# Attention with head mixing and two MLPs: score rows twelve partitions apart, one DMA a head, and first-chunk moves on GpSimd's queue

## The chip, the cores and the metric

The kernel runs on one core of one Trainium2 chip. The metric is the device time of one execution in microseconds (us). The kernel before took 1219.67 us (median of three runs, 1219.64 to 1219.95).

## The reference

All data is float32; `scale` is 1/8.

```python
q, k, v: [4, 12, 448, 64]; w_pre, w_post: [12, 12]
scores = einsum('bhij,hg->bgij', scale * q @ k^T, w_pre)
attn = exp(scores - max(scores)); attn = attn / (sum(attn) + 1e-09)
o = einsum('bhij,hg->bgij', attn, w_post) @ v
x = o as [1792, 768]
y = ((x @ w1) * (x @ w2)) @ w3 @ w_out
h = y @ w_in;  return maximum(0.01 * h, h) @ w_out2
```

Both mixes run over the twelve heads: each mixed score is a sum over heads of the scores at the same place.

## The kernel before, in words

The attention comes first. The 448 query rows of each of the four batches are cut in chunks of 120, 120, 120 and 88, sixteen chunks in all (`order`). A chunk is worked in groups of two blocks; a block is ten query rows with all twelve heads, 120 of 128 partitions.

For each chunk and pair of heads, `qk` (L222) makes the scores on TensorE (L242) into two PSUM banks. Its inner `out` copies them to a tile `s` (L254 on VectorE, L256 on ScalarE) and calls `move` (L269) for each head: a DMA (L281) that takes a head's 120 rows from `s` to the tile `sr` (`rows_of`), where the rows of one block lie in one column slot: ten query rows, each with its heads side by side. In `sr`, query row i of head h lies on partition h + 13 i (`GAP`), save that head 11's last five rows begin again at partition 64, as 11 + 117 would be 128. So head 11 takes two DMAs and every other head one. The tile `s` is one tile for all heads in the first chunk; for the others there are five buffers in turn, one a pair of heads (L232). There are three `sr` tiles, taken in turn.

The mixing matrix `kpre` has the weights of `w_pre` for the five query rows of each half of 64 partitions; `premix` (L304, matmul L315) multiplies it with two column slots of `sr`. Partitions that hold no score must be finite, so `constants_load` (L150) clears the three `sr` tiles by memset, two on GpSimd and one, the first chunk's, on VectorE (L152). `constants` (L158) makes the masks of `kpre` and `kpost` from an identity.

Then, per step k of two groups: `tops` (L320, maxima by VectorE, L325), `softmax` (ScalarE, exp with the sum, L332), `weigh` (L337: VectorE's reciprocal, then the scaling of four blocks by that, three on GpSimd and one on VectorE, L348), `postmix` of the step before (L369) with VectorE's transposes (L384), `av` (L401, products px with v, two pairs of heads a step, four where many wait), and the premix of the next two groups. Scores are made `LEAD` = 10 groups ahead. The schedule is written by hand: each engine runs its instructions in the program's order, and each DMA is issued by the engine named, in that engine's order.

The start stands at L443 to L466. Ten pairs of heads (six of the first chunk, four of the second) go through `qk` with `early` set, so that ScalarE and VectorE share the copies. The first chunk's moves are made in halves, column slots 0 to 5 and 6 to 11 (`half`). Their issuing queues: first halves of even heads by ScalarE, of odd heads by SyncE (L260); second halves of odd heads by SyncE (L460), with the loads of the third chunk's q among them, those of even heads by GpSimd (L465). All later moves are SyncE's (L263). Between them TensorE runs matmuls on a tile of ones (`turn`, L302). After the first step SyncE loads the first batch's v, six DMAs (`v_load`, L219, called at L552).

After the attention come the two MLPs, TensorE work almost alone, in which nothing is changed. The host lays out the inputs (`kernel`); the rows of `w_pre` follow the layout of `sr`.

```python
    LEAD, GAP = 10, 13
    out=dst[r0:r0 + GAP * (n - 1) + 1:GAP, n0:n0 + w, :], in_=t[i0 * w:(i0 + n) * w, :]
    shares = (nc.scalar, nc.scalar, nc.gpsimd, nc.scalar) if last else (nc.gpsimd,) * 3 + (nc.vector,)
```

Of the kernel before, what the change touches and what calls it, by code (L numbers as in the profile page):

```python
# [12 lines left out]
ALU = mybir.AluOpType  # L13
# [9 lines left out]
def attention_moe_kernel(ctx: ExitStack, tc, qt, kt, vt, w_pre, w_post, w1, w2, w3t, w_out, w_in2, w_out2, out):  # L23
# [18 lines left out]
    IB = 10  # L42
    LEAD, GAP = 10, 13
    CH = qt.shape[-1]
# [73 lines left out]
    def attention(seam):  # L118
        with ExitStack() as es, ExitStack() as left:
# [22 lines left out]
            spare = spare.bitcast(F32)  # L142
            ident, ones, eye = (spare[:, n * P:n * P + w] for n, w in ((0, P), (1, P), (2, HQ * GAP)))
            mask = spare[:, 3 * P:3 * P + 2 * HQ].rearrange("p (n i) -> p n i", i=HQ)
# [5 lines left out]
            def constants_load():  # L150
                for i, t in sorted(rows_of.items()):
                    (nc.gpsimd if i else nc.vector).memset(t, 0.0)  # L152
                for t in (kpre, kpost, eye):
                    nc.gpsimd.memset(t, 0.0)
                for n, w in enumerate((w_pre, w_post)):
                    nc.sync.dma_start(out=wrep[:, n, :], in_=w)

            def constants():  # L158
                nc.vector.tensor_tensor(out=eye[:, :Q], in0=ident[:, :Q], in1=ident[:, Q:], op=ALU.add)
                for n, gap in enumerate((GAP, H)):  # L160
                    t = eye[:, :HQ * gap].rearrange("p (i h) -> p i h", h=gap)[:, :, :H]
                    nc.vector.tensor_reduce(out=mask[:, n], in_=t, axis=AX.X, op=ALU.max)
                nc.vector.tensor_scalar(
                    out=wrep[:, 0, :], in0=wrep[:, 0, :], scalar1=scale, scalar2=None, op0=ALU.mult
                )
                nc.vector.tensor_tensor(
                    out=kpre[:, :HR].rearrange("p (i h) -> p i h", h=H),
                    in0=mask[:, 0].unsqueeze(2).to_broadcast([P, HQ, H]),
                    in1=wrep[:, 0, :].unsqueeze(1).to_broadcast([P, HQ, H]), op=ALU.mult,
                )  # L170
                for c in range(2):
                    nc.vector.tensor_tensor(
                        out=kpost[:, c, :HH * HQ].rearrange("p (h i) -> p h i", i=HQ),
                        in0=mask[:, 1].unsqueeze(1).to_broadcast([P, HH, HQ]),
                        in1=wrep[:, 1, c * HH:(c + 1) * HH].unsqueeze(2).to_broadcast([P, HH, HQ]), op=ALU.mult,
                    )
# [42 lines left out]
            def v_load(b, p):  # L219
                nc.sync.dma_start(out=vs[:, p], in_=vt[b, p])  # L220

            def qk(b, c, p, early=False):  # L222
# [28 lines left out]
                def out():  # L251
                    for e in range(2):
                        if early and (e or (b, c) == order[0] and p % 2):
                            nc.vector.tensor_copy(t[:m, e, :], pq[e][:m])  # L254
                        else:
                            nc.scalar.activation(out=t[:m, e, :], in_=pq[e][:m], func=ACTF.Copy)  # L256
                    for e in range(2):
                        args = srt[b, c], t[:m, e, :], 2 * p + e
                        if (b, c) == order[0]:
                            move(*args, nc.sync if e else nc.scalar, 0)  # L260
                            second.append(args)
                        else:
                            move(*args, nc.sync)  # L263
# [5 lines left out]
            def move(dst, t, h, queue, half=None):  # L269

                m = t.shape[0]
                n0, w = 0, m // IB
                if half is not None:
                    m, w = m // 2, w // 2
                    n0, t = half * w, t[half * m:(half + 1) * m]
                if h < H - 1:
                    parts = [(h, 0, 2 * HQ)]
                else:
                    parts = [(h, 0, HQ), (Q, HQ, HQ)]
                for r0, i0, n in parts:  # L280
                    ends["sync"] = queue.dma_start(  # L281
                        out=dst[r0:r0 + GAP * (n - 1) + 1:GAP, n0:n0 + w, :], in_=t[i0 * w:(i0 + n) * w, :]
                    )

# [165 lines left out]
            turn(13)  # L450
            queued = []
            for k in range(LEAD):
# [4 lines left out]
                if k == 5:  # L457
                    constants()
                    for args in second[1::2]:
                        move(*args, nc.sync, 1)  # L460
                        if not queued and args[-1] > 4:
                            queued.append([q_load(*order[2], a) for a in range(2)])
                if k in (7, 9):
                    for args in second[(k - 7) * 3:][:6:2]:
                        move(*args, nc.gpsimd, 1)  # L465
            turn(6)  # L466

# [38 lines left out]
            for k in range(0, NG + 2, 2):  # L506
# [42 lines left out]
                do(k // 2, upper)  # L549
                if not k:  # L550
                    for p in range(NPAIR):
                        v_load(0, p)  # L552
                for g in done:
# [580 lines left out]
```

## Time and profile before

| | |
|---|---|
| median of the runs | 1219.67 us (1219.64 to 1219.95) |
| the profiled execution's own time | 1218.51 us |
| its span, first to last instruction | 1216.7 us |
| mean granted clock of TensorE | 0.997 |
| TensorE busy | 1198.3 us (98%) |
| VectorE busy | 885.7 us (73%) |
| ScalarE busy | 550.5 us (45%) |
| GpSimd busy | 213.0 us (18%) |

The profile is one execution; its times count from the first instruction. In its rows PE is TensorE's matmuls, PEld its weight loads, DVE VectorE, ACT ScalarE, POOL GpSimd, SP SyncE; a q behind the name is the engine's sequencer, which issues DMAs. L281 is line 281 of the kernel before. "sr<-s" reads: writes sr, from s. The idle time in brackets is that of the engine just before the row, with what ended it. Busy shares are means over stages with different limits; TensorE's matmuls are pipelined and their ends modelled, so that a busy TensorE may still be slowed.

### The profile page before, as it was taken

How to read it: one execution, taken by the hardware profiler on the slowest of the kernel's cores; microseconds unless marked ns; L12 is line 12 of the kernel's file. 1: busy time of each engine (PE TensorE's matmuls, PEld its weight loads, DVE VectorE, ACT ScalarE, POOL GpSimd, SP SyncE). 2: the span in 40 equal slices, each digit the busy share in tenths (PEclk: the TensorE clock that was granted, in tenths of full speed). 3: DMA queues.
4: the chain of work that ended last, by engine and by line, in shares of the span. 5: the costliest groups of instructions: out<-in, count | busy, mean ns of one | idle time of the engine just before them, and what ended most of it. 6: DMA issues, size and time to landing. Idle time of an engine off the chain costs nothing.

```text
span 1216.7 us, 22474 instructions
## 1 busy us (share of the span) xinstructions
PE 1198.3 (98%) x8782; PEld 986.5 (81%) x8782; DVE 885.7 (73%) x1525; ACT 550.5 (45%) x1118; POOL 213.0 (18%) x169
## 2 busy tenths in 40 slices
PE   8999999999999999999999999999999999999998
PEld 5355555555579999998899999999999999999998
DVE  5687787888889988547895868567776657476572
ACT  3677776866655454323454342352233334323120
POOL 5566767666410000000000000000000000000000
PEclk9999999999999999999999999999999999999999
DMA  6767867756867756589674626063342221212012
GB/s 198 235 197 205 219 188 209 207 169 186 262 222 254 241 177 189 171 288 352 217 240 136 221 92 207 27 221 115 95 131 65 65 70 52 72 34 73 26 53 91
DMA packets 135998, 196.82 MB, mean 162 GB/s; under 512 B 26724, under 2 KB 115036, under 8 KB 135892
## 3 DMA queue, kind: packets, MB, share of 16 engines
q1 hardware_dynamic: 132048, 192.72, 49.8%
q10 hardware_dynamic: 3556, 2.02, 0.6%
q8 instruction: 69, 1.13, 0.4%
q0 software_dynamic: 288, 0.65, 0.2%
q14 instruction: 37, 0.30, 0.1%
HBM read 114.57 MB, written 42.07 MB: 129 GB/s over the span
## 4 chain that ended last, share of the span: by engine, by line
PE 84%; DVE 8%; ACT 4%; DMA 3%; issue 1%; ACTq 0%; POOL 0%; SPq 0%; DVEq 0%; POOLq 0%
PE pm L597 29%; PE po L611 19%; PE pp L908 17%; DVE ap L384 6%; PE px L401 6%; PE pw L669 6%; PE po L369 4%; ACT e L332 3%; DMA sr<-s 3%; PE pq L242 2%; PE pm L315 2%; DVE mx L325 1%; PE turn L302 1%; ACT s L256 0%; DVE e L348 0%
## 5 line engine op out<-in xcount | busy, mean ns | idle before, releaser
L597 PE MATMUL pm<-x,ws 128*128 128x384 f32 (+1 forms) x1152 | 233.9, 364 | 0.0
L597 PEld LDWEIGHTS pm<-x,ws 128*128 128x128 f32 x1152 | 208.7, 188 | 24.5 <-issue 0.6
L348 POOL TENSOR_SCALAR e<-e,sm 128x448 f32<-128x448 f32 x128 | 184.5, 1454 | 132.6 <-DVE sm L342 116.0
L332 ACT ACTIVATE e<-pm,mx 128x448 f32<-128x448 f32 x180 | 111.7, 632 | 78.2 <-DVE mx L325 71.6
L384 DVE STREAM_TRANSPOSE ap<-po 128x512 f32<-128x512 f32 (+3 forms) x216 | 115.8, 594 | 24.7 <-PE po L369 24.1
L908 PE MATMUL pp<-t,w 128*128 128x448 f32 x576 | 124.5, 368 | 0.0
L611 PE MATMUL po<-ws,g 128*128 128x384 f32 x672 | 117.2, 334 | 0.0
L611 PE MATMUL po<-wo,g 128*128 128x384 f32 x672 | 117.2, 334 | 0.0
L908 PEld LDWEIGHTS pp<-t,w 128*128 128x128 f32 x576 | 108.1, 188 | 10.9
L611 PEld LDWEIGHTS po<-wo,g 128*128 128x128 f32 x672 | 116.6, 188 | 0.2
L611 PEld LDWEIGHTS po<-ws,g 128*128 128x128 f32 x672 | 116.6, 188 | 0.0
L325 DVE TENSOR_REDUCE mx<-pm 128x1 f32<-128x448 f32 x180 | 98.6, 603 | 8.9 <-PE pm L315 8.9
L100 ACT ACTIVATE wc<-wr 128x768 f32<-128x768 f32 (+1 forms) x72 | 61.7, 859 | 87.5 <-DMA wr<-in_moe_w_dram 33.6
L908 PE MATMUL pp<-b,w 128*128 128x448 f32 x432 | 95.6, 368 | 0.0
L401 PEld LDWEIGHTS px<-ap,vs 96*64 96x64 f32 (+1 forms) x1536 | 77.7, 136 | 22.0 <-ACT e L332 16.3
L618 DVE TENSOR_TENSOR acc<-po,acc 128x384 f32<-128x384 f32 x84 | 45.4, 554 | 66.9 <-PE po L611 66.8
L256 ACT ACTIVATE s<-pq 120x448 f32<-120x448 f32 (+1 forms) x179 | 83.1, 561 | 18.2 <-PE pq L242 9.9
L315 PE MATMUL pm<-sr,kpre 64*64 64x448 f32 x720 | 84.0, 554 | 7.0 <-DMA sr<-s 5.1
L401 PE MATMUL px<-ap,vs 96*64 96x120 f32 (+3 forms) x1536 | 87.6, 266 | 3.0 <-ACT e L332 1.3
L369 PE MATMUL po<-e,kpost 64*32 64x512 f32 (+1 forms) x1472 | 89.2, 586 | 1.4 <-POOL e L348 1.2
L908 PEld LDWEIGHTS pp<-b,w 128*128 128x128 f32 x432 | 81.0, 188 | 8.0
L72 ACT ACTIVATE ws<-wc 128x768 fp32r<-128x768 f32 (+1 forms) x64 | 49.7, 788 | 69.6 <-PE po L611 45.2
(106 smaller groups left out, 1577.5 us busy)
## 6 DMA issues: line engine op xcount, KB each, us to landing
sr<-s SPq DMA_DIRECT2D x121, 210.0 KB
wr<-in_moe_w_out_dram SPq DMA_DIRECT2D x24, 768.0 KB
wr<-in_moe_w_dram SPq DMA_DIRECT2D x16, 768.0 KB
wr<-in_moe_w_in_dram SPq DMA_DIRECT2D x16, 768.0 KB
wr<-in_moe_w_dram SPq DMA_DIRECT2D x16, 512.0 KB
sr<-s SPq DMA_DIRECT2D x44, 157.5 KB
vs<-in_v_dram SPq DMA_DIRECT2D x24, 256.0 KB
kept_w<-wc SPq DMA_DIRECT2D x16, 384.0 KB
```

What stands on the lines that cost most here:

```text
L256: nc.scalar.activation(out=t[:m, e, :], in_=pq[e][:m], func=ACTF.Copy)
L315: nc.tensor.matmul(pms[ns[s % len(ns)]][half:half + Q], kpre[rows], sr[rows, 2 * t + g, :], start=True, stop=True,)
L325: nc.vector.tensor_reduce(out=mxs[n], in_=pms[n], axis=AX.X, op=ALU.max, negate=True)
L332: ends["act"] = nc.scalar.activation(out=e[:, i], in_=pms.pop(n), func=ACTF.Exp, bias=mxs.pop(n), scale=1.0, accum_out=sm[:, i:i + 1])
L348: ends["dve" if eng is nc.vector else "pool"] = eng.tensor_scalar(out=e[:, i], in0=e[:, i], scalar1=rc[:, i:i + 1], scalar2=None, op0=ALU.mult
L369: nc.tensor.matmul(po[g][32 * r:32 * (r + 1), :m], kpost[rows, x], e[rows, :m, JS[r]:JS[r] + P], start=True, stop=True,)
L384: ends["dve"] = nc.vector.transpose(out=dst, in_=po[g][:, i0:i1])
L401: nc.tensor.matmul(px[e * D:(e + 1) * D, r, :nw].rearrange("p (n i) -> p n i", i=HQ), vs[rows, p, jc, e, :], ap[rows, x, :ns, jc, h * HQ:( ...
L597: nc.tensor.matmul(dst, wt[:, a, kk, :], x[kk][:, c, c0:c0 + w], start=(i == 0), stop=(i == len(steps) - 1))
L611: nc.tensor.matmul(po, g[m][:, a, t * P:(t + 1) * P], wts[m][:, c, cs], start=(m == 0 and j == 0), stop=(m == FQ - 1 and j == 2),)
L669: nc.tensor.matmul(pw, wt[:, x, kk, :], wos[kk][y][:, cs], start=(kk == 0 and j == 0), stop=(kk == KF - 1 and j == 2),)
L908: nc.tensor.matmul(dst, w[:, i, a, kk, :], b[:, kk, c, :], start=(kk == 0 and j == 0), stop=(kk == KH - 1 and j == 2),)
```

## The change

Query row i of head h now lies on partition 4 + h + 12 i (`SKIP` = 4), from 4 to 123, so that rows 0 to 4 fall in the lower half of 64 partitions and rows 5 to 9 in the upper one without an exception: every head is one DMA. Only partitions 0 to 3 and 124 to 127 hold no score. The first chunk's `sr` tile is still cleared whole by VectorE; the other two get those eight partitions by four DMAs from it, issued by GpSimd, in place of GpSimd's two memsets. The masks are made from two shifted slices of the identity.

In the first chunk, even heads' first halves go by GpSimd's queue instead of ScalarE's, all second halves by GpSimd's queue, after the constants, and the loads of the third chunk's q follow on SyncE without moves among them. ScalarE now copies one head of every early pair, VectorE the other. The first batch's v is loaded by GpSimd, three DMAs after each of the first two steps; later batches' v as before by SyncE.

```diff
-    LEAD, GAP = 10, 13
+    LEAD, SKIP = 10, 4
...
             def constants_load():
-                for i, t in sorted(rows_of.items()):
-                    (nc.gpsimd if i else nc.vector).memset(t, 0.0)
-                for t in (kpre, kpost, eye):
+                nc.vector.memset(rows_of[0], 0.0)
+                for t in (kpre, kpost):
                     nc.gpsimd.memset(t, 0.0)
+                for i in (1, 2):
+                    for r in (slice(0, SKIP), slice(P - SKIP, P)):
+                        nc.gpsimd.dma_start(out=rows_of[i][r], in_=rows_of[0][r])
                 for n, w in enumerate((w_pre, w_post)):
                     nc.sync.dma_start(out=wrep[:, n, :], in_=w)
 
             def constants():
-                nc.vector.tensor_tensor(out=eye[:, :Q], in0=ident[:, :Q], in1=ident[:, Q:], op=ALU.add)
-                for n, gap in enumerate((GAP, H)):
-                    t = eye[:, :HQ * gap].rearrange("p (i h) -> p i h", h=gap)[:, :, :H]
-                    nc.vector.tensor_reduce(out=mask[:, n], in_=t, axis=AX.X, op=ALU.max)
+                for n, c in enumerate((SKIP, 0)):
+                    t = eyes[:, n * Q:n * Q + HR]
+                    nc.vector.tensor_tensor(
+                        out=t, in0=ident[:, c:c + HR], in1=ident[:, Q:Q + HR], op=ALU.add
+                    )
+                    nc.vector.tensor_reduce(
+                        out=mask[:, n], in_=t.rearrange("p (i h) -> p i h", h=H), axis=AX.X, op=ALU.max
+                    )
...
             def v_load(b, p):
-                nc.sync.dma_start(out=vs[:, p], in_=vt[b, p])
+                (nc.sync if b else nc.gpsimd).dma_start(out=vs[:, p], in_=vt[b, p])
...
-                        if early and (e or (b, c) == order[0] and p % 2):
+                        if early and e:
                             nc.vector.tensor_copy(t[:m, e, :], pq[e][:m])
...
-                            move(*args, nc.sync if e else nc.scalar, 0)
+                            move(*args, nc.sync if e else nc.gpsimd, 0)
...
-                if h < H - 1:
-                    parts = [(h, 0, 2 * HQ)]
-                else:
-                    parts = [(h, 0, HQ), (Q, HQ, HQ)]
-                for r0, i0, n in parts:
-                    ends["sync"] = queue.dma_start(
-                        out=dst[r0:r0 + GAP * (n - 1) + 1:GAP, n0:n0 + w, :], in_=t[i0 * w:(i0 + n) * w, :]
-                    )
+                ends["sync"] = queue.dma_start(out=dst[SKIP + h:SKIP + h + H * (IB - 1) + 1:H, n0:n0 + w, :], in_=t)
...
                 if k == 5:
                     constants()
-                    for args in second[1::2]:
-                        move(*args, nc.sync, 1)
-                        if not queued and args[-1] > 4:
-                            queued.append([q_load(*order[2], a) for a in range(2)])
-                if k in (7, 9):
-                    for args in second[(k - 7) * 3:][:6:2]:
+                    for args in second:
                         move(*args, nc.gpsimd, 1)
+                    for a in range(2):
+                        q_load(*order[2], a)
...
-                if not k:
-                    for p in range(NPAIR):
-                        v_load(0, p)
+                if k < 4:
+                    for p in range(HN):
+                        v_load(0, k // 2 * HN + p)
...
-    rows = [(p % 64 % 13 - p // 64) % 12 for p in range(128)]
+    rows = [(p - 4 if p < 64 else p - 64) % 12 for p in range(128)]
```

## Rows read from the trace of the kernel before

**Rows 1.** The page: the span, and the chain that ended last, by engine.

```profile
span 1216.7 us, 22474 instructions
...
PE 84%; DVE 8%; ACT 4%; DMA 3%; issue 1%; ACTq 0%; POOL 0%; SPq 0%; DVEq 0%; POOLq 0%
```

**Rows 2.** The chain of waits, start to 80 us: start us, us, what.

```profile
34.59 6.74 DMA sr<-s
...
42.33 6.67 DMA sr<-s
```

**Rows 3.** TensorE's timeline, 6 to 75 us: start us, us, instructions, idle before.

```profile
9.16 6.28 PE L242 MATMUL pq<-k,q 64*120 64x448 f32 x32
16.44 1.60 PE L302 MATMUL turn<-spare 128*128 128x128 f32 x12 [1.00 <-ACT s L256]
21.08 1.85 PE L315 MATMUL pm<-sr,kpre 64*64 64x448 f32 x16 [3.03 <-DMA sr<-s]
...
26.54 1.74 PE L315 MATMUL pm<-sr,kpre 64*64 64x448 f32 x16
...
46.78 0.98 PE L315 MATMUL pm<-sr,kpre 64*64 64x448 f32 x8
49.70 2.19 PE L315 MATMUL pm<-sr,kpre 64*64 64x448 f32 x8 [1.94 <-ACT s L256]
...
54.33 1.95 PE L401 MATMUL px<-ap,vs 96*64 96x120 f32 x32
```

**Rows 4.** ScalarE's timeline, 6 to 75 us.

```profile
29.16 0.98 ACT L256 ACTIVATE s<-pq 120x448 f32<-120x448 f32 x2 [2.97 <-DMA sr<-s]
...
49.11 0.98 ACT L256 ACTIVATE s<-pq 120x448 f32<-120x448 f32 x2 [2.53 <-DMA sr<-s]
```

**Rows 5.** SyncE's timeline, 15.9 to 16.6, 0 to 60, 38.9 to 41.6 us.

```profile
15.96 0.72 SPq L281 DMA_DIRECT2D sr<-s  x1
...
35.39 3.29 SPq L220 DMA_DIRECT2D vs<-in_v_dram  x6
...
41.41 0.82 SPq L281 DMA_DIRECT2D sr<-s  x1
```

**Rows 6.** GpSimd's timeline, start to 60 us.

```profile
10.54 2.39 POOL L281 DMA_DIRECT2D sr<-s  x4
...
25.93 4.33 POOL L348 TENSOR_SCALAR e<-e,sm 128x448 f32<-128x448 f32 x3 [11.36 <-ACT s L256]
33.18 4.35 POOL L348 TENSOR_SCALAR e<-e,sm 128x448 f32<-128x448 f32 x3 [2.92 <-ACT s L256]
39.77 4.35 POOL L348 TENSOR_SCALAR e<-e,sm 128x448 f32<-128x448 f32 x3 [2.25 <-DVE sm L342]
```

**Rows 7.** VectorE's timeline, start to 75 us.

```profile
2.06 4.54 DVE L152 MEMSET sr<- 128x5376 f32 x1 [1.07 <-issue]
...
27.56 2.22 DVE L325 TENSOR_REDUCE mx<-pm 128x1 f32<-128x448 f32 x4 [1.33 <-PE pm L315]
...
35.84 2.18 DVE L325 TENSOR_REDUCE mx<-pm 128x1 f32<-128x448 f32 x4
...
42.44 2.18 DVE L325 TENSOR_REDUCE mx<-pm 128x1 f32<-128x448 f32 x4
...
46.60 2.50 DVE L384 STREAM_TRANSPOSE ap<-po 128x512 f32<-128x512 f32 x4
```

**Rows 8.** Tile sr to 45 us: issue ns min/median/max; landing of GpSimd's moves.

```profile
L281 SPq DMA_DIRECT2D sr<-s x31: 717/756/1147, 8.1 to 44.1; - x31
...
L281 POOL DMA_DIRECT2D sr<-s x6: 553/553/746, 10.5 to 14.0; - x6
...
DMA to landing us min/median/max: 3.8/4.9/5.8
```

**Rows 9.** Stretches: us, busy of PE, PEld, DVE, ACT, POOL; clock; DMA; GB/s.

```profile
50.20:53.50 3.30, 3.30 (x14) 0.97 (x12) 1.32 (x3) 2.57 (x8) 0.51 (x1) 0.50 0.96 248
```

**Rows 10.** TensorE's timeline, 141 to 147 us.

```profile
144.46 1.94 PE L315 MATMUL pm<-sr,kpre 64*64 64x448 f32 x8 [1.71 <-DMA sr<-s]
```

More of the change, by code (lines that the diff above doesn't have):

```diff
@@ L142, in attention @@
             spare = spare.bitcast(F32)
-            ident, ones, eye = (spare[:, n * P:n * P + w] for n, w in ((0, P), (1, P), (2, HQ * GAP)))
+            ident, ones, eyes = (spare[:, n * P:(n + 1) * P] for n in range(3))
             mask = spare[:, 3 * P:3 * P + 2 * HQ].rearrange("p (n i) -> p n i", i=HQ)
@@ L450, in attention @@
             turn(13)
-            queued = []
             for k in range(LEAD):
```

## The prediction

> **What bounds it now.** I read the page first: a span of 1216.7 us whose last chain of waits is 84% TensorE, with 3% on the transfers sr<-s, the moves that the change rewrites [rows 1]. Then the chain itself: nearly all of that 3% lies in the first 50 us, where it runs through single moves of 6.74 and 6.67 us [rows 2]. Then TensorE's timeline [rows 3]: a gap of 3.03 us before the first premix at 21.08, ended by a move, and one of 1.94 us at 49.70, ended by a score copy of ScalarE. ScalarE's rows tell why those copies were late: the ones at 29.16 and 49.11 waited 2.97 and 2.53 us for moves, because their buffers s (five of them) were still being read [rows 4]. From 54.33 on TensorE runs nearly without gaps, so what is won or lost up to there stays to the end. The price of the whole change is thus the time at which the first A·V product (px) starts.
>
> Why the moves are late is read from SyncE's rows [rows 5]: the second half of head 11's first-half move is issued at 15.96, the last of twelve heads; the six v loads hold the queue from 35.39 for 3.29 us; and the moves of the third chunk start at 41.41, only when the move of 34.59 has landed (34.59 + 6.74 [rows 2]).
>
> **The change, part by part.**
>
> *Clearing the rows.* GpSimd's two memsets go (before them its first move could not be issued ahead of 10.54 [rows 6]); VectorE's memset ends at 2.06 + 4.54 = 6.60 [rows 7], and behind that wait GpSimd issues four small clears, at 0.553 us each, 0.746 the slowest [rows 8]: 6.6 to 8.9 or 9.6. Queued behind them are the even heads' moves. The added VectorE operation among the constants and the narrower masks cost nothing: VectorE then waits for the premix.
>
> *First halves (a).* The score steps take 6.28 us for eight pairs [rows 3], 0.785 each, so heads 10 and 11 leave TensorE at 9.16 + 4 x 0.785 = 12.3. ScalarE, which no longer issues moves, copies head 10 by 12.9, and GpSimd issues it by 13.4; SyncE issues head 11, one DMA now, at 0.756 [rows 8], by 13.7. The last issue of before ended at 15.96 + 0.72 = 16.68 and let the premix start 4.4 us later. GpSimd's moves landed 3.8 to 5.8 us after issue began [rows 8], which gives 16.7 to 18.7 for head 10; head 11 with the old 4.4 gives 18.1. TensorE itself is free at about 15.44 + 1.60 = 17.0, the end of the score steps and the warming turns [rows 3]. Bounds: 17.0 (4.1 gained) and 21.08 (nothing). I take 18.6, nearer to the landing rows, as the clears and the following second halves share the transfer engines: **2.5 us gained**.
>
> *Second halves (b).* Twelve issues behind 13.4, 6.6 us: GpSimd is free at 20.0 (22.4 at 0.746 each), before the first scaling, which comes 4.85 us after the premix (21.08 to 25.93 [rows 3, 6]), so at 23.4. The last one lands 4.9 to 5.8 us after its issue began at 19.5, 24.4 to 25.3. Group 3's premix, the first to need it, is the second half of the stretch at 26.54 [rows 3], some 5.9 us after the first premix, so 24.5. Bounds: no wait, and 3.1 us (22.4 - 0.7 + 5.8 = 27.5, less 24.5). I take **0.7 us lost**.
>
> *Second chunk's moves (c).* SyncE loses nine issues of second halves (head 11's last is two) and begins the second chunk's moves by about 15 instead of 24. Buffer s is then free when ScalarE wants it. VectorE's maxima start 8.28 us apart there (27.56, 35.84), against 6.60 in the next step (35.84, 42.44) [rows 7]: **1.7 us gained**, bounds nothing and the whole wait of 2.97 [rows 4].
>
> *Third chunk's moves (d).* With the v loads gone from SyncE and the second chunk's moves nine issues earlier, the move behind the wait at 49.11 goes out soon after its copy. Without the wait, TensorE would go from 46.78 through a premix of 1.74 and two score steps (1.57) to the first px at 50.1; it came to it at 54.33 [rows 3]. That is 4.2 us: 1.94 of idling, then a stretch of 3.30 us at a granted clock of 0.50, so at 1.2 GHz, after that idling, which costs 1.65 [rows 9], and copies that came late. I take **4.0 gained**; bounds nothing and 4.2.
>
> *v by GpSimd (e).* Three loads go behind each of the first two scalings. A v load cost SyncE 3.29 / 6 = 0.55 us [rows 5]; GpSimd's price for one is in no row. From below it is 0.55. From above, by bytes from a 105 KB move (0.553), 256 KB give 1.35; by destination rows, 128 against 10, 7.1. GpSimd has idle time: 1.2 us between the first scaling's end (30.26 [rows 6]) and the second's start (33.18) less the 1.7 of (c); 2.25 in the next step [rows 6]; and some 1.1 us before VectorE's transposes at 46.60 [rows 7] need the product of what it scaled. So six loads cost 6v - 4.5. At 0.55 that is nothing, at 1.35 it is 3.6. I take 1.0, between the two near ends: **1.5 us lost**; the far end is a rival below.
>
> *Later chunks (f).* One DMA fewer in each of the 15 later chunks saves SyncE 0.756 us of issue, beside other work. A later premix waits 1.71 us for a move at 144.46 [rows 10]; I leave it as it is. Bounds: gone, or twice as long. Row spacing 12 for 13 alters no matmul: the premix keeps its 64 x 64 tiles.
>
> Sum: 2.5 - 0.7 + 1.7 + 4.0 - 1.5 = 6.0 us. The profiled execution took 1218.51 us, its span 1216.7; so 1212.5 for it, and with the 1.16 by which the median of the runs (1219.67) lies above it, **1213.7 us**.
>
> **Rivals.** *The transfer engines, not the queues, set when the first halves land.* Then (a) and (b) are nothing, while (c) and (d), which hang on the order in SyncE's queue, stay: 1.7 + 4.0 - 1.5 = 4.2, so 1215.5. For it: in that stretch landings took 5.8 us at worst against 3.8 at best [rows 8]. Against: the last issue at 15.96 [rows 5]. Chance 0.15. The Trainium skill has a rule for this (DMA: Bandwidth & Descriptors, "Issuing engines are not separate DMA queues"): all issuing engines end at the same 16 DMA engines, so spreading saves only issue time. By that rule the time would be this rival's, if no issue were late; the landings speak for the rule, the issue at 15.96 against it.
>
> *The buffers s stay full.* The second chunk's moves now run beside GpSimd's second halves and may land no earlier; (c) and (d) are then nothing: 2.5 - 0.7 - 1.5 = 0.3, so 1219.4. Against: SyncE starts them some 9 us earlier, and the buffer is wanted only 5 us after the first premix. Chance 0.1.
>
> *Slower: v loads hold GpSimd.* If a load costs v, the six take 6v - 4.5 from the scaling and TensorE's postmix waits behind it. The point of decision is the gain without (e), 7.5: 6v - 4.5 = 7.5 at v = 2.0 us. Midway (as a ratio) between the price by bytes, 1.35, and by rows, 7.1, lies 3.1: 14.1 lost, 6.6 net, so 1226.3. For it: GpSimd's queue does nothing else while it issues. Against: its 105 KB moves cost 0.553, less than SyncE's 0.756 for the same kind. Chance 0.12.
>
> *Nothing gets behind and TensorE waits for nothing:* 4.1 + 1.7 + 4.0 = 9.8, so 1209.9. Chance 0.08.
>
> **How the numbers follow.** The forecast has 0.55. About 0.2% (2.4 us) is what a measurement of this kernel can tell from no change. Faster by more: the forecast, the first and the last rival, 0.78 less a little for their edges, 0.76. The same: the full buffers and those edges, 0.11. Slower: 0.13. The range runs from 1209.5, just under the case in which nothing is lost, to 1219.5, the full buffers, and leaves out the slow case and some of the bounds of (f).
>
> **What would show it.** Right: the first premix at 18 to 19 instead of 21.08; no wait of ScalarE's score copies on sr<-s; no stretch at half clock near 50; first px near 48, from 54.33; GpSimd's v loads at about 1 us. Wrong: GpSimd busy with issues past 24; the premix of group 3 late by several us; postmix matmuls waiting for the scaling e in the first three steps; a new wait of a copy on a buffer s; or a gap and a half-speed stretch that only moved.

## The result and the profile after

| | before | after |
|---|---|---|
| median of runs on one chip (us) | 1219.66 | 1231.1 |
| lowest to highest, six runs each | 1217.09 to 1220.26 | 1228.54 to 1232.53 |
| profiled execution; its span | 1218.51; 1216.7 | 1230.9; 1229.1 |

The change makes the kernel **slower**, by 0.9% and clear of noise: the ratio is 1.0094, with a 95% interval of 1.0079 to 1.0108. The forecast was 1213.7, with a range of 1209.5 to 1219.5.

The loss lies where the gain was looked for, in the first 63 us, and a part of it further on. The page, to set beside [rows 1]: the moves' share of the chain is a point larger.

```profile
span 1229.1 us, 22449 instructions
...
PE 82%; DVE 8%; DMA 4%; ACT 4%; SPq 1%; POOL 1%; issue 1%; ACTq 0%; DVEq 0%; POOLq 0%
```

TensorE's timeline of the changed kernel, 6 to 75 us, to set beside [rows 3].

```profile
8.93 6.28 PE L248 MATMUL pq<-k,q 64*120 64x448 f32 x32
15.13 1.60 PE L301 MATMUL turn<-spare 128*128 128x128 f32 x12
27.92 3.26 PE L314 MATMUL pm<-sr,kpre 64*64 64x448 f32 x16 [11.18 <-DMA sr<-s]
...
35.49 0.98 PE L314 MATMUL pm<-sr,kpre 64*64 64x448 f32 x8
37.54 0.98 PE L314 MATMUL pm<-sr,kpre 64*64 64x448 f32 x8 [1.06 <-ACT s L262]
...
52.48 2.76 PE L314 MATMUL pm<-sr,kpre 64*64 64x448 f32 x16 [4.27 <-DMA q<-in_q_dram]
...
62.70 1.95 PE L400 MATMUL px<-ap,vs 96*64 96x120 f32 x32
```

The score steps and warming turns are done a little sooner than before (16.7 against 18.0), and then TensorE waits 11.18 us for a move, where it waited 3.03. The first premix starts at 27.92 instead of 21.08, 6.8 us late. In that wait the clock falls to half, 1.2 GHz, and stays there for 13.7 us; the columns of this row of stretches are those of [rows 9].

```profile
18.90:32.60 13.70, 4.68 (x20) 1.69 (x22) 2.31 (x4) 2.07 (x7) 6.62 (x12) 0.50 0.71 173
```

At 52.48 a second wait of 4.27 us stands. The row names a load of q, which a premix does not read; it waited for the second chunk's last move, which by the trace's completion events was issued at 40.27 and landed at 52.02. The first px starts at 62.70, 8.4 us behind the 54.33 of before.

GpSimd's timeline of the changed kernel, to set beside [rows 6].

```profile
6.91 2.30 POOL L156 DMA_DIRECT2D sr<-sr  x4 [5.43 <-DVE sr L151]
9.20 1.21 POOL L282 DMA_DIRECT2D sr<-s  x2
...
14.43 0.56 POOL L282 DMA_DIRECT2D sr<-s  x1 [2.31 <-ACT s L262]
17.49 0.56 POOL L282 DMA_DIRECT2D sr<-s  x1 [2.50 <-DMA sr<-sr]
19.11 0.56 POOL L282 DMA_DIRECT2D sr<-s  x1 [1.06 <-DMA sr<-sr]
22.70 4.54 POOL L282 DMA_DIRECT2D sr<-s  x8 [3.04 <-DMA sr<-sr]
...
29.70 0.56 POOL L282 DMA_DIRECT2D sr<-s  x1 [0.57 <-DMA sr<-s]
33.81 4.34 POOL L347 TENSOR_SCALAR e<-e,sm 128x448 f32<-128x448 f32 x3 [3.56 <-ACT s L262]
38.12 1.73 POOL L226 DMA_DIRECT2D vs<-in_v_dram  x3
...
45.44 1.66 POOL L226 DMA_DIRECT2D vs<-in_v_dram  x3
```

The four clears (sr<-sr) are issued when the forecast had them. What follows is not: GpSimd itself waits for **clears to land**. In the trace its DMAs use eight completion counters in turn, so the ninth has to wait for the first, the tenth for the second. Its issues at 14.43, 17.49, 19.11 and 22.70 come right behind the landings of the four clears, at 13.80, 16.86, 18.83 and 22.08 (the row at 14.43 names a score copy, but head 8's had ended by 12.02). The view of the clears' line has the time from issue to landing: 6.9 us for the first clear, 13.4 for the last.

```profile
L156 POOL DMA_DIRECT2D sr<-sr x4: 521/536/730, 6.9 to 8.7; - x4
...
DMA to landing us min/median/max: 6.9/9.9/13.4
```

SyncE's timeline, to set beside [rows 5]: six first halves take 15.27 us to issue.

```profile
7.88 15.27 SPq L282 DMA_DIRECT2D sr<-s  x6
23.20 2.13 SPq L206 DMA_DIRECT2D q<-in_q_dram  x2
25.43 15.59 SPq L282 DMA_DIRECT2D sr<-s  x12
```

Nearly all of it is the issues themselves: 1.00, 2.76, 4.64, 3.28, 1.53 and 1.56 us, where [rows 8] have a median of 0.756. The worst stands in the tile sr's row.

```profile
L282 SPq DMA_DIRECT2D sr<-s x186: 755/756/4638, 7.9 to 328.7; - x186
```

So a queue that the clears are not on is late as well, and it is this queue that the premix waits for in the end: by the completion events SyncE's last first half, issued at 21.58, lands at 27.79, GpSimd's last at 25.04. ScalarE's score copies wait a little less than before, 2.27 and 0.96 us where [rows 4] has 2.97 and 2.53, and it is no gain.

```profile
36.34 0.98 ACT L262 ACTIVATE s<-pq 120x448 f32<-120x448 f32 x2 [2.27 <-DMA sr<-s]
...
48.90 0.98 ACT L262 ACTIVATE s<-pq 120x448 f32<-120x448 f32 x2 [0.96 <-DMA sr<-s]
```

Later, the wait that [rows 10] show with 1.71 us has 4.92 here: that premix starts at 156.04 instead of 144.46, so the lag of 8.4 us has grown to 11.6, of the 12.4 that the spans differ by.

```profile
156.04 1.88 PE L314 MATMUL pm<-sr,kpre 64*64 64x448 f32 x8 [4.92 <-DMA q<-in_q_dram]
```

### The profile page after: what moved, and what is told of

Its sections match the earlier page's. It is cut to its first block, busy times and chain, and to the rows that moved or that the text cites. A ratio compares the mean times of both kernels' runs of the same rounds, so it can differ in the third digit from the quotient of the medians.

```text
span 1229.1 us, 22449 instructions
## 1 busy us (share of the span) xinstructions
PE 1197.8 (97%) x8782; PEld 985.8 (80%) x8782; DVE 884.7 (72%) x1523; ACT 552.6 (45%) x1121; POOL 216.4 (18%) x188
## 4 chain that ended last, share of the span: by engine, by line
PE 82%; DVE 8%; DMA 4%; ACT 4%; SPq 1%; POOL 1%; issue 1%; ACTq 0%; DVEq 0%; POOLq 0%
PE pm L592 29%; PE po L606 19%; PE pp L903 17%; PE pw L664 6%; DVE ap L383 5%; PE px L400 5%; PE po L368 3%; ACT e L331 3%; DMA sr<-s 3%; PE pq L248 1%; PE pm L314 1%; DVE mx L324 1%; DMA vs<-in_v_dram 1%; POOL e L347 1%; SPq L282 1%
## 5 line engine op out<-in xcount | busy, mean ns | idle before, releaser
L324 DVE TENSOR_REDUCE mx<-pm 128x1 f32<-128x448 f32 x180 | 98.6, 603 | 25.4 <-PE pm L314 25.4
L314 PE MATMUL pm<-sr,kpre 64*64 64x448 f32 x720 | 83.8, 569 | 21.4 <-DMA sr<-s 11.2
L262 ACT ACTIVATE s<-pq 120x448 f32<-120x448 f32 (+1 forms) x182 | 85.0, 561 | 11.6 <-PE pq L248 8.3
L314 PEld LDWEIGHTS pm<-sr,kpre 64*64 64x64 f32 x720 | 25.2, 135 | 78.9 <-issue 34.8
```

The source lines that it names most:

```text
L314: nc.tensor.matmul(pms[ns[s % len(ns)]][half:half + Q], kpre[rows], sr[rows, 2 * t + g, :], start=True, stop=True,)
L324: nc.vector.tensor_reduce(out=mxs[n], in_=pms[n], axis=AX.X, op=ALU.max, negate=True)
```

## Experiments

Times are medians; the kernel before, run beside each, had 1218.6 to 1220.3. The runs stand on several chips, each beside the kernel before; a ratio is to that kernel. A single run of these kernels strays by some 5 us either way, at worst by 11, so a single profile shows an order of events, and the medians and intervals show the price.

**The clears taken out.** The changed kernel, with GpSimd's whole memsets of before in their place.

```
-for i in (1, 2):
-    for r in (slice(0, SKIP), slice(P - SKIP, P)):
-        nc.gpsimd.dma_start(out=rows_of[i][r], in_=rows_of[0][r])
+for i, t in sorted(rows_of.items()):
+    (nc.gpsimd if i else nc.vector).memset(t, 0.0)
```

> The change with GpSimd's two whole memsets back in place of the four clears; all else as changed. Theory A (the four clears, whose rows of 21.5 KB landed 3 us apart at 13.8 to 22.1 us, hold the few transfer engines that carry them, and the first moves wait behind): GpSimd starts its moves at 10.5, the first premix at 19 to 21 us instead of 27.9, SyncE's six first moves issue in about 6 us instead of 15.3, and the kernel takes 1218 to 1224. Rival B (moves by GpSimd's queue land late by themselves): first premix at 26 us or later, 1229 or more.

1222.4 us, ratio 1.0024 (0.9999 to 1.005). Its TensorE timeline:

```profile
22.88 3.27 PE L312 MATMUL pm<-sr,kpre 64*64 64x448 f32 x16 [6.43 <-DMA sr<-s]
...
47.81 3.27 PE L312 MATMUL pm<-sr,kpre 64*64 64x448 f32 x16 [4.60 <-DMA q<-in_q_dram]
```

Without the clears 8.7 of the 11.4 us are gone, although the memsets hold GpSimd until 10.4 again. That is theory A by the time and by SyncE's six issues (6.20 us); the first premix, at 22.88, is later than the 19 to 21 expected. What is left of the change still gains nothing.

**The clears later.** The same four, issued behind the twelve second halves.

```
-for i in (1, 2):                                    # in constants_load
-    for r in (slice(0, SKIP), slice(P - SKIP, P)):
-        nc.gpsimd.dma_start(out=rows_of[i][r], in_=rows_of[0][r])
...
 for args in second:
     move(*args, nc.gpsimd, 1)
+for i in (1, 2):
+    for r in (slice(0, SKIP), slice(P - SKIP, P)):
+        nc.gpsimd.dma_start(out=rows_of[i][r], in_=rows_of[0][r])
```

> The change with the same four clears issued behind the twelve second halves. Theory A: the first premix at 17.5 to 20 us, since GpSimd's moves start at 6.6 and no large row is ahead of them; the clears then hold some engines from about 21 to 34 and the second chunk's moves land late there, so the time is 1220 to 1228. Rival B: first premix still after 25 us, time 1229 or more.

1231.59 us, ratio 1.0085 (1.0061 to 1.011).

```profile
20.75 3.27 PE L311 MATMUL pm<-sr,kpre 64*64 64x448 f32 x16 [3.61 <-DMA sr<-s]
...
46.64 2.19 PE L311 MATMUL pm<-sr,kpre 64*64 64x448 f32 x8 [4.28 <-ACT s L259]
56.91 3.14 PE L311 MATMUL pm<-sr,kpre 64*64 64x448 f32 x16 [3.67 <-DMA sr<-s]
```

The first premix is as early as before (20.75; expected 17.5 to 20), and the price has only moved: the later premixes now wait for score copies and for moves. At 1231.59 it is dearer than theory A's 1220 to 1228, and the profiled run, of 1235.4, is the slowest of its seven. The loss goes with the clears, and not with their being first in the queue.

**Row spacing and one DMA a head alone.** The kernel before, with nothing else of the change (memsets and queues as before).

> The kernel before with the new row spacing and one DMA a head alone; memsets, queues and v loads as before. Theory C (with head 11 in one DMA, all ten transfer engines of a move carry every head, and the one that lands last, which the two half DMAs of head 11 did not use, gets later where transfers are dense): the wait of 1.71 us before the premix at 144 grows by 2 to 4 us, 1221 to 1225. Rival D (the later wait in the changed kernel comes from its other parts): that wait is 0 to 2 us, 1217 to 1220.

1216.68 us, ratio 0.9973 (0.9953 to 0.9992). Measured again, beside other kernels:

> The new row spacing with one DMA a head and nothing else, once more, on the same chip as the three beside it: 1215.5 to 1218 by the first measurement (1216.68); if the gain there was a matter of the chip or of chance, 1219 to 1221.

1217.04 us, ratio 0.9984 (0.9967 to 1.0). TensorE's timeline of the second measurement, and then SyncE's row for head 11's first half, the last that SyncE issues:

```profile
21.21 3.03 PE L312 MATMUL pm<-sr,kpre 64*64 64x448 f32 x16 [3.60 <-DMA sr<-s]
...
50.63 1.95 PE L398 MATMUL px<-ap,vs 96*64 96x120 f32 x32 [0.36 <-ACT e L329]
```

```profile
13.21 0.89 SPq L280 DMA_DIRECT2D sr<-s  x1
```

SyncE's last first half goes out 2.75 us sooner than before (13.21 against 15.96 [rows 5]) and ScalarE's 0.56 us sooner (13.52 against 14.08), yet the first premix is where it was: the issues did not set it. The first px comes at 50.63 instead of 54.33. This small part gains some 3 us by both medians (the second interval just reaches 1.0) and is the version to keep, below both kernels. Whether the spacing or the single DMA does it was not separated.

The wait near 144 us fits neither theory C nor rival D: it is 3.49 us in the first measurement's profile and 3.42 in the second's. The first profile's run took 1223.43 us, the longest of its ten, although its first px comes as early, at 50.73; it has a wait near 124 us that the second lacks.

```profile
123.83 1.88 PE L312 MATMUL pm<-sr,kpre 64*64 64x448 f32 x8 [2.46 <-ACT e L329]
```

So a part of the scatter of single runs arises behind the stretch that these experiments alter.

**One queue at a time, on top of that.** v by GpSimd; even heads' first halves by GpSimd (with ScalarE and VectorE sharing the copies as in the changed kernel); all second halves by GpSimd; and v left on SyncE, but three loads after each of the first two steps. One line of each of the first three:

```
+(nc.sync if b else nc.gpsimd).dma_start(out=vs[:, p], in_=vt[b, p])      # v
+move(*args, nc.sync if e else nc.gpsimd, 0)                              # first halves
+for args in second:                                                      # second halves
+    move(*args, nc.gpsimd, 1)
```

> The new row spacing with one DMA a head (1216.68 us when run alone), and beside it only the loads of v moved: three after each of the first two steps, on GpSimd's queue. Left in the first stages after the clears are taken away: 5.7 us (1222.4 less 1216.7), shared by three changes of queue. Theory E (the first halves on GpSimd's queue cost it): this move costs nothing, 1215.5 to 1218. Theory F (v on GpSimd holds up its multiplications and lands late): 1219 or more, with a wait for v ahead of the first output products near 51. Theory G (the moves of the third chunk, freed from the v loads ahead of them on SyncE, come sooner): 1213 to 1215.5, without a wait near 150.

> The new row spacing with one DMA a head, and beside it only the even heads' first halves on GpSimd's queue instead of ScalarE's, with ScalarE and VectorE sharing the copies as in the changed kernel. Theory E (GpSimd's first halves start behind its memsets at 10.4 and share the transfer engines with SyncE's): the first group mixed starts at 23 or later, and the time is 1219 to 1223. Theory F or H (the cost lies with v or with the second halves): first group mixed at 21.4 or before, 1215 to 1218.

> The new row spacing with one DMA a head, and beside it only all twelve second halves on GpSimd's queue, the third chunk's q loads behind them. Theory H (twelve second halves in one burst from GpSimd hold transfer engines while the second chunk's moves run): the third and fourth pair of groups mixed wait 3 us or more, and the time is 1219 to 1223. Theory E: no loss, 1214 to 1218, since SyncE's queue gets free of six issues of 0.7 us each and the second chunk's moves come sooner.

> The new row spacing with one DMA a head, the loads of v kept on SyncE's queue but three after each of the first two steps. If three loads less ahead of the third chunk's moves matter (theory G): 1213 to 1216, below the layout alone (1216.68). If not: the same within 2 us. If the later three v loads land too late for the first output products: 1218 or more.

| on top of the layout (1217.04) | us | ratio, 95% |
|---|---|---|
| v by GpSimd | 1219.07 | 1.0 (0.998 to 1.0021) |
| even first halves by GpSimd | 1216.91 | 0.9986 (0.9973 to 1.0) |
| all second halves by GpSimd | 1221.16 | 1.0013 (1.0 to 1.0026) |
| v by SyncE, three and three | 1217.2 | 0.9992 (0.9976 to 1.0008) |

The first halves cost nothing that the medians show, and theory E falls by the time; the first premix, at 22.67, lies between what the two sides expected, but it is at 22.56 with v in threes too, where nothing ahead of it is altered. Three v loads fewer ahead of the third chunk's moves gain nothing (theory G falls). The second halves cost 4 us, though not where theory H put it: not at the later premixes but at the first.

```profile
25.21 3.26 PE L312 MATMUL pm<-sr,kpre 64*64 64x448 f32 x16 [7.11 <-DMA q<-in_q_dram]
```

Eight of the second halves were issued between 10.45 and 15.04, beside the first halves, and the premix waits 7.11 us instead of 3.60. With v by GpSimd the wait is later:

```profile
43.46 3.27 PE L312 MATMUL pm<-sr,kpre 64*64 64x448 f32 x16 [3.36 <-DMA sr<-s]
```

The loads, issued from 31.06 on while the second chunk's last moves were still to go, took 6 to 10 us to land. With the v loads on SyncE behind those moves, the same premix has no wait. Of the seven kernels here with v on GpSimd, six wait 3 us or more for moves or copies ahead of the first px at this step; of the twelve with v on SyncE, none. By the medians v costs 2 us, which the intervals do not tell from nothing.

**Everything but the clears and the second halves.** The kernel of the first experiment, its second halves put back as before.

> The changed kernel without its clears (whole memsets instead; 1222.4 us) and without the second halves' move to GpSimd (odd heads' by SyncE, even heads' by GpSimd in two groups, q loads among them, as before). What stays is the row spacing, one DMA a head, even heads' first halves and v by GpSimd. If the parts add up (1217.0 for the spacing; v 2.0 more, first halves 0.1 less): 1218.9, between 1217 and 1220.5. If the second halves cost only in company of the other moves: 1217 or less; if v and the first halves cost more together than alone: 1221 or more.

1221.51 us, ratio 1.0012 (0.999 to 1.0033): above the sum of the parts, which the interval still takes in, and hardly below the 1222.4 that has the second halves as well. In the profiles the first px is at 54.68 here, as with v alone (54.66), and at 58.61 with the second halves too, but the times do not bear that out. How the 5 us left without the clears are shared between v and the second halves is thus not settled; alone, the second halves cost more.

**The second halves held back.** The layout alone, with a copy on GpSimd that waits until all first halves have landed, ahead of its six second halves.

```
+if k == 7:
+    nc.gpsimd.tensor_copy(kpost[:, 1, 31:], rows_of[0][:, 0, :1])
```

> The new row spacing with one DMA a head (1216.7 us), GpSimd's six second halves held back by a copy of one column that waits until all first halves have landed (the copy writes a column of the second mixing weights that nothing reads). If second halves that run beside the first halves share out the transfer engines and so delay the first group mixed (theory H, by which twelve of them at once cost 4.5 us): the first group mixed starts at 20.5 or before (21.4 without) and the time is 1213.5 to 1216. If the transfers are not short of engines there: 21.4, and 1216 to 1218. If the held second halves come too late for the fourth pair of groups: a wait there near 33 to 36, and 1218 or more.

1221.78 us, ratio 1.002 (1.0002 to 1.0039). TensorE's timeline:

```profile
18.22 1.73 PE L312 MATMUL pm<-sr,kpre 64*64 64x448 f32 x16 [1.87 <-DMA sr<-s]
23.56 0.98 PE L312 MATMUL pm<-sr,kpre 64*64 64x448 f32 x8
29.14 1.77 PE L312 MATMUL pm<-sr,kpre 64*64 64x448 f32 x8 [4.59 <-DMA sr<-s]
```

With no second halves of GpSimd beside them, the first halves are in by 18.2, three us sooner (20.5 or before was expected), so the transfers do share something that is short. But the held ones are then 4.59 us late for group 3, and the time is not the 1213.5 to 1216 hoped for but that of the third case. Here a transfer is gained only at the price of another.

**The clears alone.** The layout alone, its memsets kept, with the four clears added behind them: transfers that nothing needs soon.

> The kernel before with the new row spacing and one DMA a head (1216.7 us), its queues as they were (first halves by ScalarE and SyncE, GpSimd's six second halves), its memsets kept, and the four clears added on GpSimd's queue behind its memsets at 10.4, as so many transfers more that nothing waits for soon. Theory A1 (the clears hold transfer engines that all queues share): ScalarE's and SyncE's first halves wait too, the first group mixed starts at 24 or later (21.4 without), and the time is 1221 to 1226. Rival A2 (only what stands behind them on GpSimd's own queue waits): the first group mixed at 21 to 22.5, only GpSimd's second halves late, and the time within 2 us of 1216.7.

1228.12 us, ratio 1.0069 (1.0049 to 1.0089): 11 us for four DMAs with nothing behind them in their queue but GpSimd's six second halves, and dearer than even theory A1 had it (24 or later, 1221 to 1226). TensorE's and ScalarE's timelines:

```profile
33.20 3.27 PE L315 MATMUL pm<-sr,kpre 64*64 64x448 f32 x16 [8.51 <-DMA q<-in_q_dram]
```

```profile
10.90 3.84 ACTq L283 DMA_DIRECT2D sr<-s  x2
14.79 0.54 ACT L263 ACTIVATE s<-pq 120x448 f32<-120x448 f32 x1 [3.92 <-DVE spare L170]
15.36 5.76 ACTq L283 DMA_DIRECT2D sr<-s  x2
```

ScalarE needs 5.76 us to issue two moves (0.8 each without the clears), and its copies wait behind them. That is theory A1: what the clears hold, all queues use. The Trainium skill (DMA: Bandwidth & Descriptors, "Issuing engines are not separate DMA queues") has the DMAs of all issuing engines run, interleaved, on the same 16 DMA engines; this trace agrees, with ScalarE's queue slow beside GpSimd's clears.

**What is it that they hold?** Six variants of the clears' shape in the changed kernel or in the clears alone: eight DMAs of two rows 124 apart; four rows in 48 pieces of 1.8 KB; sixteen DMAs of one row each in sixteen pieces; then the same bytes read from 48 partitions, written to 48 partitions, and both.

> The change with the same 32 rows cleared by eight DMAs of two rows that lie 124 partitions apart, instead of four DMAs of four neighbouring rows. If neighbouring rows share a path and are slow for that (four rows of 21.5 KB in 3 us): the clears land about 1 us apart, done by 16 to 18 us, first premix at 21 to 24 us. If it is the bytes on a few engines alone: two engines now carry what four did, the clears end at 30 us or later, first premix after 32.

1229.44 us in its one run, first premix at 28.53. The early clears landed 1.2 us apart, but the last at 22.26, as before; neither expectation is met. (The rows are sixteen, not the expectation's 32.)

> The changed kernel (1231.1 us) with the same four clears by GpSimd, of the same bytes, but read from one row of zeros over and over, so that each is 48 descriptors of 1.8 KB and not four of 21.5 KB. Theory A (four descriptors of 21.5 KB hold the few transfer engines that they fall to, 2 to 4 us each, and what is queued there waits): the clears land within 5 us of their issue, the first group mixed starts at 23 or before instead of 27.9, and the time comes to what whole memsets gave, 1221 to 1224. Rival B (it is GpSimd's queue: four DMAs more ahead of its first halves, whatever their form): the first group mixed stays past 26 and the time above 1228.

1226.14 us, ratio 1.0069 (1.0043 to 1.0095). The clears landed after 9.5 to 10.7 us, and the first premix of the profiled run, the slowest of its six with 1233.91, is no earlier, 28.13. Neither theory is met: the premix is rival B's, the time between the two. By the medians cutting them up is worth 5 us, but the interval overlaps that of the changed kernel.

> The kernel of the clears alone (new row spacing, one DMA a head, memsets kept, clears added as transfers that nothing waits for soon; 1228.12 us, first group mixed at 33.2), with the same 344 KB cleared by sixteen DMAs of one row each, cut into sixteen pieces of 1.3 KB. Theory A3 (a clear of four rows runs on four of the sixteen transfer engines, and SyncE's and ScalarE's first halves need those four too): spread over all, 344 KB are some 2 us at the 180 GB/s that the first stages moved, so the first group mixed starts at 21.4 to 24 and the time is 1217 to 1220.5, with up to 2 us more where sixteen issues of 0.55 us hold GpSimd's second halves back. Theory P (rows 0 to 3 and 124 to 127 are the narrow place, whatever engine writes there): first group mixed at 28 or later, 1225 or more. The Trainium skill, page DMA: Bandwidth & Descriptors, section Why a DMA increments its semaphore by 16 and not by 1, has the number of engines as the largest up to 16 that divides the outermost size of both sides: four for the clears as they stand in the change, sixteen here.

1228.54 us, ratio 1.0071 (1.0047 to 1.0095): nothing gained on 1228.12, although the profile's first premix, at 26.93, is 6.3 us earlier (theory P had 28 or later). The stretch from 12 to 16 us of this kernel, and then of the layout alone (second measurement):

```profile
12.00:16.00 4.00, 2.70 (x16) 1.03 (x12) 3.82 (x14) 0.43 (x1) 3.00 (x7) 1.00 0.92 85
```

```profile
12.00:16.00 4.00, 2.81 (x16) 1.12 (x12) 3.82 (x14) 1.13 (x3) 1.94 (x4) 1.00 0.77 217
```

The transfer engines are busier, 0.92 against 0.77, and move 85 GB/s against 217. So it is not that few of them work: together they are busier and move less, which speaks against theory A3.

> The kernel of the clears alone again (1228.12 us; first group mixed at 33.2 where it is 21.2 without them), its four clears now read from 48 partitions of zeros (1.8 KB of each) and written, as before, into rows 0 to 3 and 124 to 127. Spreading them over sixteen engines changed nothing (1228.54 us; engines 92% busy at 85 GB/s from 12 to 16 us), so the narrow place is the few rows. Theory PW (few rows written): the first group mixed at 26 or later, 1225 or more. Theory PR (few rows read): 21 to 23.5, and 1217 to 1219.5. Rival Q (the place of the clears in GpSimd's queue, whatever rows they touch): 26 or later here and in the run beside it. The Trainium skill, page SBUF — State Buffer, section Door 1: The DMA port swizzle, has rows 0 to 3 on one of sixteen ports and 124 to 127 on another, each port at some 27 GB/s; by that, 86 KB take 3.2 us through one port, an estimate.

> The same four transfers of 86 KB, read from rows 0 to 3 and 124 to 127 of the first chunk's tile, and written into 48 partitions each of a scratch tile that nothing reads: no row of the tiles is cleared by them (whole memsets do that). Theory PW (few rows written are the narrow place): the first group mixed at 21 to 23.5, and 1217 to 1219.5. Theory PR (few rows read): 26 or later, 1225 or more. Theory both, or Q: 26 or later in both runs.

> The same four transfers of 86 KB at the same place of GpSimd's queue, read from 48 partitions and written into 48 partitions (of v's tile, which v's loads overwrite later); no row of the tiles is cleared by them (whole memsets do that). Reading few rows alone and writing few rows alone both kept the first group mixed at 29 (1223.57 and 1226.47 us). Theory N (few rows on either side are the narrow place): 21 to 24 here, and 1217 to 1220.5. Rival Q (four more transfers at this place of GpSimd's queue cost it, whatever rows they touch): 27 or later, 1223 or more.

| 344 KB more from GpSimd's queue | their landing, us | first premix | 12 to 16, 16 to 20 us, GB/s | us | ratio, 95% |
|---|---|---|---|---|---|
| none (layout alone) | | 21.2 | 217, 197 | 1217.04 | 0.9984 (0.9967 to 1.0) |
| 48 rows to 48 rows | 3.0 to 5.6 | 25.4 | 175, 182 | 1222.27 | 1.0023 (1.0003 to 1.0042) |
| 48 rows to 4 rows | 8.8 to 10.6 | 28.9 | 132, 64 | 1223.57 | 1.0041 (1.0022 to 1.006) |
| 4 rows to 48 rows | 11.2 to 11.6 | 29.1 | 103, 79 | 1226.47 | 1.0057 (1.0036 to 1.0078) |
| 4 rows to 4 rows (the clears) | 7.6 to 15.7 | 33.2 | 145, 117 | 1228.12 | 1.0069 (1.0049 to 1.0089) |

```profile
12.00:16.00 4.00, 3.40 (x18) 1.41 (x16) 3.82 (x14) 0.54 (x1) 4.00 (x8) 1.00 0.82 175
16.00:20.00 4.00, 1.40 (x10) 0.63 (x6) 1.86 (x4) 1.03 (x3) 0.83 (x2) 1.00 0.84 182
```

These two rows are those of 48 rows to 48. Few rows on either side delay the first premix by 3.6 to 3.8 us more than as many bytes spread over 48 rows, and on both sides by 7.8. But spread out they are not free either: the run lies between what the two theories expected (25.4, 1222.27). So by the medians about half of the 11 us is that **344 KB more are moved at this place at all**, and about half that they go **from and to few rows**. Of these four, neighbours in the table lie inside each other's intervals in time; the extremes do not. The landings say the same: 3.0 to 5.6 us when both sides are wide, 7.6 to 15.7 when either has four rows.

The Trainium skill (SBUF — State Buffer, "Door 1: The DMA port swizzle") has rows 0 to 3 on one port and 124 to 127 on another, and by its rate of a port 86 KB take 3.2 us, an estimate from that page. The 3.06, 1.97 and 3.25 us between the landings in the changed kernel are near it, but do not show it: the clears go to the two groups of rows in turn, so by two ports they could overlap, and eight DMAs with one row of each group ended at the same time as four with four rows (22.26 and 22.08). No run here shows the ports themselves, and why few rows are slow stays open.

All these transfers came from GpSimd's queue; no run issues them from another, so a part of that queue in their price is not excluded. Why 344 KB in 48 rows cost 5 us where 217 GB/s would move them in 1.6 (worked out from the layout's row above) stays open too; part is the half clock, which, worked out from the granted clocks of its 4 us stretches, lasts 10 us in that run's profile against 3.4 without them.

## Why the prediction was wrong, step by step

**Clearing the rows** is the step that failed. It priced the four clears by their issue, "at 0.553 us each", and took what follows as queued behind 8.9. Issued they were, by 9.2. But as transfers they lasted until 22.08, and the moves beside and behind them were late: 8.7 us of the time by the first experiment, 11 when added to a kernel that did not need them. A memset was exchanged for transfers in a stretch in which transfers set the time. Only the issue was costed; for the transfers themselves (a) merely took 18.6 instead of 17.0.

**(a) First halves.** Forecast: first premix at 18.6, bounds 17.0 and 21.08; measured 27.92. The upper bound, "nothing", was wrong in kind: the landings of [rows 8] were read as a property of the queue, to which nothing could be lost. The first four even heads went out about as forecast; head 10, due on GpSimd by 13.4, went out at 17.49, and SyncE's last, due by 13.7, was done at 23.1. Nor did sooner issues gain anything without the clears: (a) hung the premix on the issue at 15.96, and the layout alone has SyncE's last first half out at 13.21 with the premix at 21.21, where it was. Only fewer transfers beside the first halves brought it forward, to 18.22.

**(b) Second halves.** Forecast 0.7 lost, for a late group 3. Alone they lose 4, and in the first premix, since GpSimd issues them beside the first halves that are still under way. In company of the rest the loss is not told apart (1221.51 against 1222.4). (A slip in the sum: by [rows 3] group 3 is 6.3 us behind the first premix, 26.54 + 0.87 - 21.08, not 5.9.)

**(c) Second chunk's moves.** Forecast: SyncE starts them by 15, a gain of 1.7. They started at 25.43, behind first halves and q loads that took until 25.3. No gain. (SyncE lost seven issues of second halves, not nine; the other two were the q loads, which stay.)

**(d) Third chunk's moves.** Forecast 4.0 gained by a first px near 50. It did not come: the second chunk's last moves were late for the premix at 52.48. But the layout alone reaches its first px at 50.63, so the 4.0 was a fair size for the gap; it belongs to the row spacing and single DMA, which the prediction had at nothing, and not to the v loads: three fewer of them ahead gave nothing, and with all of them on GpSimd's queue the first px came at 54.66.

**(e) v by GpSimd.** The size of the issue was off the other way: 1.73 / 3 = 0.58 us a load, not 1.0, so GpSimd's time was not the price. v still costs some 2 us alone by the medians, inside the noise; in the profiles the loads, freed from SyncE's order, run beside the moves that are wanted first.

**(f) Later chunks.** Left as it was; measured 4.92 us of wait for 1.71 in the profiled runs. It has 1.4 to 4.9 us in the kernels tried, 3.42 and 3.49 with the layout alone, so what part of it the change makes is open. It also limits the premise that what is won by the first px stays to the end: of the layout's 3.7 us at the first px its second profile keeps 1.2 in the span, and its first, 3.6 ahead there, ends 4.9 behind.

**The rivals.** The rival by which transfers, not queues, set the landings named the right place: (a) and (b) did hang on them, and the issue at 15.96, which spoke against it, did not set the premix. Its price, nothing gained, stopped at zero for the same reason as (a). The slower rival, v holding GpSimd, did not happen: the loads took 0.58 us, far from its point of 2.0. The full buffers came true in part: the copies at 36.34 still waited 2.27 us.

## What to carry over

A DMA that replaces a memset has to be costed as bytes on the transfer engines, and by how many rows it reads and writes, not by its issue: here 2.3 us of issue stood for 9 to 11 us of the time. In a stretch where the next step waits for a landing, a queue is also an order of priority: giving work to an idle queue lets transfers that nobody needs yet run beside those that are needed now. And a bound of "nothing lost" for a landing holds only if nothing is added beside it.

## What the hardware showed beyond that

The instruction that issues a DMA stretches when transfers are held up: on SyncE from 0.756 to 4.64 us in the changed kernel, to 7.75 with the transfers of 4 rows to 48, and on ScalarE to 7.1 there, where it stands in the way of the copies. GpSimd's own issue did not stretch (0.556 to 0.632), but it waited for landings once its eight completion counters were all out. And cut into more and smaller pieces, 344 KB to the same rows, 0 to 3 and 124 to 127, cost as much (1228.54 us against 1228.12): transfer engines 92% busy moved 85 GB/s.
